# Key weights by rows, three centred tiles and other places for the bulk loads in a transformer block's forward and backward pass

## The chip, the cores and the metric

The kernel runs on one core of a Trainium2 chip. The metric is the device time of one execution in microseconds. The core has five engines that run their own instruction streams and meet at semaphores: PE (TensorE, matmuls; its weight loads are listed as PEld), DVE (VectorE), ACT (ScalarE), POOL (GpSimd) and SP (SyncE, which here only issues transfers). Transfers are issued from SP, ACT and POOL and are moved by 16 DMA engines. A "transposing load" is a transfer that turns a matrix on its way.

## The reference

The reference computes a block of linear attention followed by a gated MLP, and the gradients of all its inputs. With x of 2048 rows and 640 columns, 32 heads of 20 columns and F = 1728:

```python
ln = layernorm(x)                         # no weights
q, k, v = split(ln @ wqkv)                # 640 x 1920
phi(t) = where(t > 0, t + 1, exp(t)) + 1e-6
kv = sum_s phi(k)_s v_s ;  z = sum_s phi(k)_s          # per head
o = phi(q) kv / (phi(q) z + 1e-6)
h = x + o @ wo
out = h + (silu(layernorm(h) @ w1) * (layernorm(h) @ w3)) @ w2
return out, and the gradients of x, wqkv, wo, w1, w3, w2 for a given grad_out
```

All inputs and outputs are bfloat16.

## The kernel before

Rows are worked on in 16 tiles of 128 (S = 16 x 128), columns in 5 tiles of 128. There is no scheduler: the order of the instructions on each engine is the order in which the program calls them, and an engine that waits holds up all that stands behind it. SP's order of transfers is fixed in the same way.

*Loads at the start.* `load_x(a, b)` loads x tiles a to b - 1 into `x_sb`, `load_wq(a, b)` loads columns 320 a to 320 b of wqkv (2 to 4 are the key weights, 0 to 2 the query weights, 4 to 6 the value weights). SP issues x 0, x 1, the first half of the key weights, x 2, the second half, x 3, x 4-5 (L115, L189 to L195), then w2 and grad_out by transposing loads (`load_w2T`, `load_g2T`, L460 and L461), x 6-9 (L462) and more.

*Pass one* (the loop at L528) takes the 16 tiles in turn. The layer norm of a tile is two BN_STATS, an aggregate and an addition on DVE (`Stats.part`, `stat`), a power on POOL (the reciprocal deviation `ln_rs`) and then the normalisation in place: on DVE (`ln1.norm`, L161), or for tiles 10, 12 and 14 on ACT (`norm_act`, L166), which also needs a bias made on POOL (L170). Tile 0 is only centred (`center_first`); its reciprocal deviation is applied as a scale in the activations (`RAW = 1`) and, later, to `x_sb` itself by `p1_scale` (L264). The tile is turned by PE transposes with a copy by ACT (`p1_tr`, tiles 0 to 7) or by a transposing load (tiles 8 to 15, issued in `p1_norm`, L251). Then PE multiplies it with the key weights: two halves of 320 columns, 5 matmuls each (`p1_half`, L268), into an accumulator `big` of which there are two. ACT takes Exp and Relu of it (`phi`, L295 and L296) into `mq` and `rq`, of which there are three each; DVE makes the feature from them (L299, L300) and thus frees them. This last step (`rest`) is kept in a list and runs later, where `v_steps` has an `R`. After tiles 6, 7, 9 and 11 query tiles 0 to 3 are made in the same way (`q_tile`).

`v_steps` is the order of DVE's work by tile: `S` statistics, `N` normalisation, `C` scaling, `R` rest; they come ahead of the tile's `phi`. `A`, `B` and `L` are normalisations after it: `A` before the query tile, `B` and `L` behind it. `trickle` names the bulk loads (w1 and w3 in pieces, `w13`) that are issued at the end of a tile, `outs` the stores. `m_part` accumulates phi(k)^T times x in spare places (L430), `ghh_chunk` makes pieces of grad_out times w2^T (L395).

*After the loop* the rest of the query tiles, the denominators (`r_prod` on POOL; `r_head` = `r_row` on DVE and `r_T`, a transposing load) and kv alternate, with bulk loads between them (L592 to L624). The list of `run` (L948) then makes Wp (the folded kv times wo, five transposing loads, L709) and the attention output by tile (`f2_half`, L657). `r_store` (L735) stores scaled queries with transfers issued from POOL.

*The backward pass* ends the weight gradient of wo in `q_parts` (L1219 to L1226), whose last products `tri` are turned by transposing loads and used at L1388. Around it SP issues `load_xnT` (the normalised x, turned, 4 pieces), `load_wqT` (wqkv turned), and at L1402 to L1415 the loads of `mN` and `pkb`. The remaining stages up to 818 us are matmuls in which PE is not held up.

Of the kernel before, what the change touches and what calls it, by code (L numbers as in the profile page):

```python
# [55 lines left out]
def kernel(  # L56
# [126 lines left out]
    def load_wq(a, b):  # L183
        dma(out=wqkv[:, :, a * HD:b * HD], in_=wq_v[:, :, a * HD:b * HD])

    def load_x(a, b):
        dma(out=x_sb[:, a:b, :], in_=xS[:, a:b, :])

    load_x(1, 2)  # L189
    A.activation(sg[:], zero[:], AF.Exp)  # L190
    load_wq(2, 3)
    load_x(2, 3)
    load_wq(3, 4)
    load_x(3, 4)
    load_x(4, 6)  # L195

# [45 lines left out]
    RAW = 1  # L242
# [23 lines left out]
    def p1_half(acc, t, n0):  # L266
        for c in range(DT):
            T.matmul(acc, lhsT=pqT[:, c, t * P:(t + 1) * P], rhs=wqkv[:, c, n0:n0 + HD], start=(c == 0),  # L268
                     stop=(c == DT - 1))

    def p1_acc():
        return ps.tile([P, 2, 512], F32, name="big", bufs=2)

    def p1_mm(t, n0, between=None, halves=None):
        acc = p1_acc() if halves is None else None
        for j in range(2):
            p1_half(acc[:, j, 0:HD] if halves is None else halves[j][:, 0:HD], t, n0 + j * HD)
            if j == 0 and between is not None:
                between()
        return acc  # L280
# [6 lines left out]
    def phi_tiles():  # L287
        return [p1.tile([P, D], BF16, name=n, bufs=3) for n in ("mq", "rq")]

    def phi(acc, dst, t, parts=None):  # L290

        mq, rq = parts or phi_tiles()
        if parts is None:
            kw = dict(scale=ln1.rs[:, t:t + 1]) if t < RAW else {}
            A.activation(two(mq[:]), acc[:, :, 0:HD], AF.Exp, **kw)  # L295
            A.activation(two(rq[:]), acc[:, :, 0:HD], AF.Relu, **kw)  # L296

        def rest():
            V.tensor_scalar(out=mq[:], in0=mq[:], scalar1=1.0, scalar2=1e-6, op0=ALU.min, op1=ALU.add)  # L299
            V.tensor_tensor(out=dst, in0=mq[:], in1=rq[:], op=ALU.add)  # L300
        held.append(rest)
# [160 lines left out]
    load_x(6, 10)  # L462
# [26 lines left out]
    warm_up(8, p1_acc()[:, 0])  # L489
    stat(1)  # L490
    p1_norm(1)
    ln1.part(x_sb, 2, 0)
    ln1.part(x_sb, 2, 1)
    ln1.part(x_sb, 3, 0)
    p1_norm(2)
# [7 lines left out]
    def load_wo():  # L503
        dma(out=wo[:], in_=A_wo.rearrange("(c p) n -> p c n", p=P))

    trickle = {4: w13[0], 5: lambda: w13[1](0, 1), 6: lambda: w13[1](1, 2), 12: w13[2]}
# [3 lines left out]
               4: (("S", 7), R, ("N", 7), ("S", 8)), 5: (R, ("N", 8), ("S", 9)), 6: (R, ("N", 9), ("S", 10)),  # L510
               7: (("S", 11), R, R, ("A", 10), ("L", 11)), 8: (("S", 12), R, R, ("S", 13)),
               9: (("N", 13), R, ("S", 14), ("B", 12)), 10: (R, R, ("S", 15)), 11: (R, ("A", 14), ("L", 15))}
# [15 lines left out]
    for t in range(ST):  # L528
        first = None
        if t < RAW:  # L530
            first = phi_tiles()
            kh = [ps.tile([P, 512], F32, name="k0", tag="m", bufs=2) for _ in range(2)]

            def act(i, j):
                A.activation(first[i][:, j * HD:(j + 1) * HD], kh[j][:, 0:HD], (AF.Exp, AF.Relu)[i],
                             scale=ln1.rs[:, t:t + 1])

            def between():
                act(0, 0)
                p1_tr(t + 1)  # L540
                act(1, 0)
            k = p1_mm(t, D, between, kh)
            act(0, 1)
            act(1, 1)
        else:
            k = p1_mm(t, D, (lambda: p1_tr(t + 1)) if t + 1 < XT_DMA else None)
        steps = v_steps.get(t, (R,) * len(held))
        for step in steps:
            if step is R:
                held.pop(0)()  # L550
            elif step[0] in V_OPS:
                V_OPS[step[0]](step[1])
        phi(k, pk_all[:, t, :], t, first)
        for when in ("A", "B", "L"):
            for step in steps:
                if step is not R and step[0] == when:
                    p1_norm(step[1])
            if when == "A" and t in QT:
                q_tile(QT.index(t))
        if 3 <= t < 7:  # L560
            ghh_chunk(t - 3, lambda: ps.tile([P, 512], F32, name="gp", tag="m", bufs=2))
        m_part(0, M0.get(t, ()))
        if t >= 11:
            V.memset(bd[:, t - 11, :], 0.0)
            make_mask(t - 11)
        if t >= 9:
            m_part(1, [2 * (t - 9), 2 * (t - 9) + 1])
        for f, *n in outs.get(t, ()):
            f(*n)
        if t in trickle:  # L570
            trickle[t]()
# [10 lines left out]
    def r_head(t):  # L582
        r_row(t)
        r_T(t)
# [7 lines left out]
    load_wq(4, 6)  # L592
    group_out(SC - 1)
    w13[3]()
# [8 lines left out]
    load_wo()  # L603
    for go in w13[4:]:
        go()
# [6 lines left out]
    r_head(1)  # L612
# [9 lines left out]
    m_end(3)  # L622
    r_T(2)
    load_w2T(4 * P, 8 * P)  # L624
# [319 lines left out]
    def kv3():  # L944
# [6 lines left out]
        (q_out, 10, 14), (mlp_ghh, 4),  # L951
        (q_late, 15), (w2_room,), (sig_table,), (f2_half, 0, 0), (f2_half, 1, 0), (f2_half, 2, 0), (f2_half, 3, 0), (mlp_ghh, 5),
        (f2_half, 0, 1), (r_store, 4, 5), (f2_half, 1, 1), (f2_hn, 0), (r_store, 5, 6), (f2_half, 2, 1), (f2_hn, 1),
# [360 lines left out]
    part(4)  # L1314
    load_xnT(2)
    part(20)
# [64 lines left out]
    load_xnT(3)  # L1381
    load_wqT(0)
# [20 lines left out]
    dma(out=mN, in_=m_v)  # L1403
    dma(out=rows(dwoT_d), in_=dwoT[:])

# [8 lines left out]
    for n in range(4):  # L1414
        load_pk(n)  # L1415
# [189 lines left out]
```

## Time and profile before

| | |
|---|---|
| Median of 3 runs | 819.58 us (819.23 to 820.79) |
| The profiled execution | 820.36 us |
| Its span on the core | 818.6 us |
| PE busy | 811.6 us (99%) |
| DVE, ACT, POOL busy | 452.7, 324.8, 131.7 us |
| DMA moved | 162.46 MB, mean 198 GB/s |

By stretch, from the same execution (engine-busy time in us):

| Stretch | PE | DVE | ACT | GB/s |
|---|---|---|---|---|
| 5 to 16 us | 10.12 of 11 | 9.29 | 9.34 | 278 |
| 16 to 28 us | 11.95 of 12 | 11.21 | 10.56 | 279 |
| 28 to 46 us | 18.00 of 18 | 15.73 | 13.96 | 191 |
| 46 to 80 us | 34.00 of 34 | 24.79 | 20.47 | 267 |
| 80 to 100 us | 19.57 of 20 | 17.51 | 13.47 | 218 |
| 558 to 568 us | 9.53 of 10 | 1.90 | 1.90 | 165 |

A profile line of the timeline holds the start in us from the span's start, the duration in us, the engine, the line of the kernel, the operation, what it writes and reads, the size, the number of instructions taken together (xN), and in brackets the engine's idle time before it and what ended it. "SPq" is SP's sequencer issuing transfers. In the list of waits the numbers are the total in us, the number of times and the longest. Matmuls are pipelined, so a line's duration runs past the start of the next; the pace is read from starts: 0.135 us for a matmul 320 wide.

### The profile page before, as it was taken

How to read it: one execution, taken by the hardware profiler on the slowest of the kernel's cores; microseconds unless marked ns; L12 is line 12 of the kernel's file. 1: busy time of each engine (PE TensorE's matmuls, PEld its weight loads, DVE VectorE, ACT ScalarE, POOL GpSimd, SP SyncE). 2: the span in 40 equal slices, each digit the busy share in tenths (PEclk: the TensorE clock that was granted, in tenths of full speed). 3: DMA queues.
4: the chain of work that ended last, by engine and by line, in shares of the span. 5: the costliest groups of instructions: out<-in, count | busy, mean ns of one | idle time of the engine just before them, and what ended most of it. 6: DMA issues, size and time to landing. Idle time of an engine off the chain costs nothing.

```text
span 818.6 us, 13711 instructions
## 1 busy us (share of the span) xinstructions
PE 811.6 (99%) x5261; PEld 501.6 (61%) x5292; DVE 452.7 (55%) x973; ACT 324.8 (40%) x609; POOL 131.7 (16%) x198
## 2 busy tenths in 40 slices
PE   9999999999999999999999999999999999999998
PEld 6777544555555555754577777777777777544444
DVE  7859997998898566300057777772781544200000
ACT  7856688665565666011112212222212334211111
POOL 2243333323222212100001111110220000000000
PEclk9999999999999999999999999999999999999999
DMA  9899899696485556999877877269994888979991
GB/s 262 207 242 277 206 276 302 207 244 174 128 209 158 169 168 168 239 254 243 233 178 181 218 194 193 58 111 181 269 217 93 179 193 153 249 175 235 221 239 37
DMA packets 335889, 162.46 MB, mean 198 GB/s; under 512 B 252560, under 2 KB 329072, under 8 KB 335824
## 3 DMA queue, kind: packets, MB, share of 16 engines
q1 hardware_dynamic: 291920, 120.68, 63.8%
q0 software_dynamic: 7328, 24.48, 8.9%
q10 hardware_dynamic: 36576, 16.42, 8.2%
q8 instruction: 41, 0.67, 0.3%
q14 instruction: 24, 0.20, 0.1%
HBM read 47.09 MB, written 53.43 MB: 123 GB/s over the span
## 4 chain that ended last, share of the span: by engine, by line
PE 96%; DMA 1%; ACT 1%; DVE 1%; issue 0%; SPq 0%; POOL 0%; DVEq 0%
PE mm L395 20%; PE job L1335 19%; PE ghn L1131 14%; PE gxn L1504 8%; PE gw L1086 7%; PE big L268 4%; PE o L913 4%; PE o L859 3%; PE gwo L1219 3%; PE macc L430 3%; PE gr L1188 3%; PE dkv L1441 3%; PE at L657 2%; DMA wqkv<-in_A_wqkv_dram 1%; PE dkv L1369 1%; DMA tri<-tri 1%
## 5 line engine op out<-in xcount | busy, mean ns | idle before, releaser
L1335 PE MATMUL job<-gb,hnN 128*128 128x496 bf16 (+3 forms) x576 | 116.8, 366 | 0.0
L1131 PEld LDWEIGHTS <-ggb 128*128 128x128 bf16 x864 | 84.5, 98 | 33.0
L395 PE MATMUL mm<-pqT,w 128*128 128x512 bf16 x396 | 93.2, 379 | 0.5
L1335 PEld LDWEIGHTS <-hnN 128*128 128x128 bf16 x576 | 55.8, 98 | 61.0
L395 PEld LDWEIGHTS <-w 128*128 128x128 bf16 x540 | 52.6, 98 | 62.9 <-issue 0.6
L1339 ACT CAST obs<-job 128x496 bf16<-128x496 f32 (+4 forms) x56 | 28.5, 510 | 123.6 <-PE job L1335 123.6
L1131 PE MATMUL ghn<-w13a,ggb 128*128 128x320 bf16 x448 | 63.5, 299 | 0.0
L1146 DVE SCALAR_TENSOR_TENSOR wb<-gs,hnb 128x640 f32<-128x640 bf16 x16 | 13.2, 825 | 88.1 <-ACT gs L1143 88.1
L1131 PE MATMUL ghn<-w13b,ggb 128*128 128x320 bf16 x416 | 61.4, 299 | 0.0
L395 PE MATMUL mm<-g2T,w2T 128*128 128x512 bf16 x228 | 58.8, 379 | 0.6
L1086 PE MATMUL gw<-hb,g 128*128 128x512 bf16 (+2 forms) x316 | 58.4, 345 | 0.2
L1086 PEld LDWEIGHTS <-g 128*128 128x128 bf16 x320 | 31.3, 98 | 27.0
L420 ACT CAST ghh<-mm 128x512 bf16<-128x512 f32 x48 | 28.2, 588 | 48.2 <-PE mm L395 41.4
L1196 POOL TENSOR_TENSOR sz<-Zb,g_h 128x640 f32<-128x640 bf16 x16 | 20.2, 1262 | 163.7 <-DVE g_h L1197 163.7
L796 ACT ACTIVATE sig<-mm 128x512 bf16<-128x512 f32 x56 | 33.7, 602 | 25.0 <-PE mm L395 21.6
L1143 ACT ACTIVATE gs<-ghn 128x640 bf16<-128x640 f32 x16 | 11.3, 705 | 76.0 <-PE ghn L1131 76.0
L395 PEld LDWEIGHTS <-w2T 128*128 128x128 bf16 x260 | 25.4, 98 | 23.4
L268 PEld LDWEIGHTS <-pqT 128*128 128x128 bf16 x320 | 30.7, 98 | 13.5 <-ACT pqT L260 0.9
L268 PE MATMUL big<-wqkv,pqT 128*128 128x320 bf16 x250 | 38.4, 299 | 0.2
L1335 PEld LDWEIGHTS <-g 128*128 128x128 bf16 x320 | 31.0, 98 | 11.5
L832 DVE TENSOR_TENSOR gate<-gate,sig 128x1024 bf16<-128x1024 bf16 x28 | 19.3, 689 | 33.9 <-ACT gate L807 31.1
L1091 ACT CAST gw2o<-gw 128x512 bf16<-128x512 f32 (+2 forms) x20 | 10.4, 519 | 66.6 <-PE gw L1086 25.3
(217 smaller groups left out, 1391.2 us busy)
## 6 DMA issues: line engine op xcount, KB each, us to landing
hh_d<-hhT SPq DMA_DIRECT2D x24, 256.0 KB, 2.8
gg_d<-gate POOLq DMA_DIRECT2D x24, 256.0 KB, 4.4
gg_d<-ghh POOLq DMA_DIRECT2D x24, 256.0 KB, 4.1
ggb<-gg_d SPq DMA_DIRECT2D x6, 896.0 KB, 5.3
ggb<-gg_d ACTq DMA_DIRECT2D x6, 832.0 KB, 5.7
ggb<-gg_d SPq DMA_DIRECT2D x2, 1728.0 KB, 13.9
pk_d<-pk_all SPq DMA_DIRECT2D x4, 640.0 KB, 5.4
g<-in_grad_out_dram SPq DMA_DIRECT2D x4, 640.0 KB, 5.7
```

The source lines that it names most:

```text
L268: T.matmul(acc, lhsT=pqT[:, c, t * P:(t + 1) * P], rhs=wqkv[:, c, n0:n0 + HD], start=(c == 0), stop=(c == DT - 1))
L395: T.matmul(acc[:], lhsT=w[:, c, fc * P:(fc + 1) * P], rhs=rhs[:, c, :], start=(c == 0), stop=(c == DT - 1))
L420: A.copy(out=ghh[n // 2][:, n % 2, :], in_=acc[:])
L430: T.matmul(macc[m][j][:, 0:n], lhsT=pk_all[:, t, m * P:(m + 1) * P], rhs=x_ext[:, t, j * HD:j * HD + n], start=(t == 0), stop=(t == ST - 1))
L796: A.activation(sig[:, i, :], gp[:], AF.Sigmoid)
L859: T.matmul(accs[i, j][:, 0:HD], lhsT=hhT[c][:, fc, i * P:(i + 1) * P], rhs=w2[:, fc, j * HD:(j + 1) * HD], start=(first and fc == 0), stop ...
L913: T.matmul(o2["ps"][:, 0:HD], lhsT=hhT[c][:, fc, i * P:(i + 1) * P], rhs=w2[:, fc, j * HD:(j + 1) * HD], start=(fc == 0), stop=(fc == FT - 1))
L1086: T.matmul(acc[:, 0:fw], lhsT=g2[:, t, m * P:(m + 1) * P], rhs=hb[b][:, t, 0:fw], start=(t == 0), stop=(t == ST - 1))
L1131: T.matmul(acc[:, j, 0:HD], lhsT=ggb[t // 2][:, k, lo:lo + P], rhs=rhs[:, j * HD:(j + 1) * HD], start=(k == 0), stop=(k == NG - 1))
L1335: T.matmul(acc[:, 0:n], lhsT=lhs[:, t, m * P:(m + 1) * P], rhs=rhs(t), start=(t == 0), stop=(t == ST - 1))
L1339: A.copy(out=ob, in_=acc[:, 0:n])
L1504: T.matmul(acc[:, j, 0:HD], lhsT=g, rhs=wqT[:, k, j * HD:(j + 1) * HD], start=(k == 0), stop=(k == 14))
```

## The change

It has seven parts.

1. The key weights come in two pieces by rows (256 and 384 rows of 640 columns; `load_wk`), both ahead of x tile 2. Tile 0's product is made row piece by row piece (`first_mm`); four warm-up matmuls after tile 0's transposes instead of eight. Tile 0's activations are taken whole.
2. Tiles 1 and 2 too are only centred (`RAW = 3`), and scaled on DVE later (`("C", 1)` and `("C", 2)` at tiles 5 and 6). In tile 1 the transposes of the next tile come after both halves (`at`).
3. x tiles 6 to 9 are loaded ahead of the transposing loads of w2 and grad_out.
4. The normalisations of tiles 12 and 14 on ACT come ahead of the activations of tiles 9 and 11 (`F`).
5. Bulk loads move: w1's second piece from tile 12 to tile 7, the value weights to tile 9, w3's second piece to tile 13, wo and the rest of w1 and w3 to the end of the loop, the second piece of w2 to where those were.
6. Query tile 1's transposing load comes after those of m's last block; r's tiles 4 and 5 are stored earlier from POOL.
7. In the backward pass the third and fourth pieces of the turned x and the query part of the turned wqkv are loaded later: behind the transposing loads of `tri`, and behind `pkb`.

```diff
+    def load_wk(a, b):
+        dma(out=wqkv[:, a:b, D:2 * D], in_=wq_v[:, a:b, D:2 * D])
     load_x(1, 2)
     A.activation(sg[:], zero[:], AF.Exp)
-    load_wq(2, 3)
+    load_wk(0, 2)
+    load_wk(2, DT)
     load_x(2, 3)
-    load_wq(3, 4)
     load_x(3, 4)
     load_x(4, 6)
+    load_x(6, 10)
...
-    RAW = 1
+    RAW = 3
...
+    def p1_mm(t, n0, between=None, at=0):
+        acc = p1_acc()
         for j in range(2):
+            p1_half(acc[:, j, 0:HD], t, n0 + j * HD)
+            if j == at and between is not None:
                 between()
         return acc

+    def first_mm(between):
+        acc = p1_acc()
+        for c in range(DT):
+            for j in range(2):
+                T.matmul(acc[:, j, 0:HD], lhsT=pqT[:, c, 0:P], rhs=wqkv[:, c, D + j * HD:D + (j + 1) * HD],
+                         start=(c == 0), stop=(c == DT - 1))
+            if c == 1:
+                between()
+        return acc
...
     load_g2T(0)
-    load_x(6, 10)
     load_w2T(2 * P, 4 * P)
...
-    warm_up(8, p1_acc()[:, 0])
-    stat(1)
-    p1_norm(1)
+    warm_up(4, p1_acc()[:, 0])
+    ln1.part(x_sb, 1, 0)
+    ln1.part(x_sb, 1, 1, lambda: center(1))
     ln1.part(x_sb, 2, 0)
-    ln1.part(x_sb, 2, 1)
+    ln1.part(x_sb, 2, 1, lambda: center(2))
     ln1.part(x_sb, 3, 0)
-    p1_norm(2)
     ln1.part(x_sb, 3, 1)
...
-    trickle = {4: w13[0], 5: lambda: w13[1](0, 1), 6: lambda: w13[1](1, 2), 12: w13[2]}
+    trickle = {4: w13[0], 5: lambda: w13[1](0, 1), 6: lambda: w13[1](1, 2), 7: w13[2], 9: lambda: load_wq(4, 6), 13: w13[3]}
...
-               4: (("S", 7), R, ("N", 7), ("S", 8)), 5: (R, ("N", 8), ("S", 9)), 6: (R, ("N", 9), ("S", 10)),
+               4: (("S", 7), R, ("N", 7), ("S", 8)), 5: (R, ("N", 8), ("S", 9), ("C", 1)), 6: (R, ("N", 9), ("S", 10), ("C", 2)),
                7: (("S", 11), R, R, ("A", 10), ("L", 11)), 8: (("S", 12), R, R, ("S", 13)),
-               9: (("N", 13), R, ("S", 14), ("B", 12)), 10: (R, R, ("S", 15)), 11: (R, ("A", 14), ("L", 15))}
+               9: (("F", 12), ("N", 13), R, ("S", 14)), 10: (R, R, ("S", 15)), 11: (("F", 14), R, ("L", 15))}
...
+        turn = (lambda: p1_tr(t + 1)) if t + 1 < XT_DMA else None
+        k = p1_mm(t, D, turn, int(t == 1)) if t else first_mm(turn)
...
+            elif step[0] == "F":
+                p1_norm(step[1])
...
-    load_wq(4, 6)
     group_out(SC - 1)
-    w13[3]()
+    load_wo()
+    for go in w13[4:]:
+        go()
     z_late((2, 3, 4), big())
...
-    load_wo()
-    for go in w13[4:]:
-        go()
+    load_w2T(4 * P, 8 * P)
...
-    r_head(1)
+    r_row(1)
...
+    r_T(1)
     r_T(2)
-    load_w2T(4 * P, 8 * P)
...
-        (q_out, 10, 14), (mlp_ghh, 4),
+        (r_store, 4, 5), (q_out, 10, 14), (r_store, 5, 6), (mlp_ghh, 4),
...
-        (f2_half, 0, 1), (r_store, 4, 5), (f2_half, 1, 1), (f2_hn, 0), (r_store, 5, 6), (f2_half, 2, 1), (f2_hn, 1),
+        (f2_half, 0, 1), (f2_half, 1, 1), (f2_hn, 0), (f2_half, 2, 1), (f2_hn, 1),
...
     part(4)
+    part(20)
     load_xnT(2)
-    part(20)
...
-    load_xnT(3)
-    load_wqT(0)
     fill(4)
...
-    dma(out=mN, in_=m_v)
-    dma(out=rows(dwoT_d), in_=dwoT[:])
...
-    for n in range(4):
-        load_pk(n)
+    load_pk(0)
+    load_pk(1)
+    dma(out=mN, in_=m_v)
+    dma(out=rows(dwoT_d), in_=dwoT[:])
+    load_pk(2)
+    load_pk(3)
+    load_xnT(3)
+    load_wqT(0)
```

More of the change, by code (lines that the diff above doesn't have):

```diff
@@ L272, in p1_acc @@
         return ps.tile([P, 2, 512], F32, name="big", bufs=2)
-    def p1_mm(t, n0, between=None, halves=None):
-        acc = p1_acc() if halves is None else None
+    def p1_mm(t, n0, between=None, at=0):
+        acc = p1_acc()
         for j in range(2):
-            p1_half(acc[:, j, 0:HD] if halves is None else halves[j][:, 0:HD], t, n0 + j * HD)
-            if j == 0 and between is not None:
+            p1_half(acc[:, j, 0:HD], t, n0 + j * HD)
[9 more added lines that the diff above has]
+            if c == 1:
                 between()
@@ L288, in phi_tiles, with phi @@
         return [p1.tile([P, D], BF16, name=n, bufs=3) for n in ("mq", "rq")]
[L290 to L296, printed above, removed]
+    def phi(acc, dst, t):
+        mq, rq = phi_tiles()
+        kw = dict(scale=ln1.rs[:, t:t + 1]) if t < RAW else {}
+        A.activation(two(mq[:]), acc[:, :, 0:HD], AF.Exp, **kw)
+        A.activation(two(rq[:]), acc[:, :, 0:HD], AF.Relu, **kw)
         def rest():
@@ L528 @@
     for t in range(ST):
[L529 to L546, printed above, removed]
+        turn = (lambda: p1_tr(t + 1)) if t + 1 < XT_DMA else None
+        k = p1_mm(t, D, turn, int(t == 1)) if t else first_mm(turn)
         steps = v_steps.get(t, (R,) * len(held))
@@ L550 @@
                 held.pop(0)()
+            elif step[0] == "F":
+                p1_norm(step[1])
             elif step[0] in V_OPS:
                 V_OPS[step[0]](step[1])
-        phi(k, pk_all[:, t, :], t, first)
+        phi(k, pk_all[:, t, :], t)
         for when in ("A", "B", "L"):
```

## The prediction

> **What bounds the kernel now.** I read the busy shares and the chain first, then the waits of PE, then timelines of the stretches that the change touches.
>
> ```profile
> PE 811.6 (99%) x5261; PEld 501.6 (61%) x5292; DVE 452.7 (55%) x973; ACT 324.8 (40%) x609; POOL 131.7 (16%) x198
> PE 96%; DMA 1%; ACT 1%; DVE 1%; issue 0%; SPq 0%; POOL 0%; DVEq 0%
> ...
> PE k L268 <- DMA wqkv<-in_A_wqkv_dram: 0.6, 2, 0.4
> PE gkvT L1388 <- DMA tri<-tri: 0.5, 1, 0.5
> PE at L657 <- DVE rden L378: 0.2, 1, 0.2
> ```
>
> PE is the bound. The change neither adds nor removes a real matmul, so it can only win where PE waits, and every microsecond by which PE is pushed back is lost for good. Waits are few: about 1.5 us before 13.5 us (two for key weights, three for a transposed x tile), 0.40 at 85.57 us and 0.63 at 566.50 us (both taken between the starts of neighbouring matmuls, which is more than the idle time in the list). That is some 2.5 us to win in 819. L657 is put down to DVE, but PE's weight loader waited there until 85.52 for a Wp block that landed at 85.48.
>
> The start, from the timeline:
>
> ```profile
> 6.61 0.84 PE L268 MATMUL k<-wqkv,pqT 128*128 128x320 bf16 x5 [0.18 <-DMA wqkv<-in_A_wqkv_dram]
> 8.14 0.84 PE L268 MATMUL k<-wqkv,pqT 128*128 128x320 bf16 x5 [0.41 <-DMA wqkv<-in_A_wqkv_dram]
> ...
> 10.94 0.45 DVE L161 TENSOR_SCALAR x_sb<-x_sb,ln_mv,ln_rs 128x640 bf16<-128x640 bf16 x1 [0.26 <-POOL ln_rs L155]
> ```
>
> See that PE waits for both halves of the key weights, and that DVE normalises tile 3 only at 10.94: PE's tile 3 starts at 12.68, and from 10.94 on DVE has no gap over 0.11 us until 35.06.
>
> Tiles 8 to 12 of pass one, ACT, POOL, DVE and PE:
>
> ```profile
> 29.15 0.70 ACT L295 ACTIVATE mq<-big 128x640 bf16<-128x640 f32 x1 [0.20 <-DVE pk_all L300]
> ...
> 32.40 0.70 ACT L295 ACTIVATE mq<-big 128x640 bf16<-128x640 f32 x1 [0.76 <-DVE pk_all L300]
> ...
> 34.84 0.92 ACT L166 ACTIVATE x_sb<-x_sb,nb,ln_rs 128x640 bf16<-128x640 bf16 x1
> ...
> 32.21 0.41 POOL L170 TENSOR_SCALAR nb<-ln_mv,ln_rs 128x1 f32<-128x1 f32 x1
> ...
> 18.16 0.38 DVE L264 TENSOR_SCALAR x_sb<-x_sb,ln_rs 128x640 bf16<-128x640 bf16 x1
> 18.46 0.88 DVE L148 BATCH_NORM_STATS2 st<-x_sb 128x6 f32<-128x320 bf16 x2
> ...
> 30.74 2.88 PE L268 MATMUL big<-wqkv,pqT 128*128 128x320 bf16 x20
> 34.27 1.52 PE L268 MATMUL big<-wqkv,pqT 128*128 128x320 bf16 x10
> 39.98 1.25 PE L268 MATMUL big<-wqkv,pqT 128*128 128x320 bf16 x8
> ```
>
> PE has no wait here, but little room. ACT's Exp waits for DVE (a pair of feature buffers of the three must be free), and PE's next tile needs the accumulator of two tiles before, of which there are two. Tile 9's Exp and Relu end at 33.70, PE wants that buffer at 34.27; the pair before it ends at 30.45 against 30.74; tile 11's ends at 39.79 against 39.98.
>
> **The change part by part.**
>
> *Start.* The two 400 KB column halves become row pieces of 320 and 480 KB, both ahead of x tile 2. Before, landing times were: x1 3.60, first half 6.57, x2 7.00, second half 8.10, x3 8.53, x4-5 9.38. At the same place in bytes x2 now lands where the second half did, 8.10. The first half took 2.97 us after x1, the second only 1.10 after x2: 1.87 us are no data time. If that excess goes with the rows of the first weight transfer (256 for 640), x2 lands at 8.10 - 1.87 x 0.6 = 6.98. Nothing here says which; I take 7.4, a bit nearer the low end, since all later transfers are then in a backlog as the second half was. The Trainium skill ("DMA: Bandwidth & Descriptors", Specifications) puts full transfer rate at pieces of 512 B and up, so rows of 640 and 1280 B would differ in nothing. By that rule x2 lands at 8.10 and the sum below is 0.70 higher; the trace agrees on the steady rate (400 KB in 1.10, 320 KB in 0.85 us) and is silent on the excess.
>
> From x2 on the work is a chain: two statistics 0.92 with the gap, aggregate 0.24, centring 0.45 (the row of the 640-wide normalisation; its step is 0.36), two statistics of x3 0.92, aggregate and epsilon 0.4, POOL's power 0.65 with its gaps, which hides x4's first statistics, normalising x3 0.45, then to PE's transposes, ACT's copy (starts 0.49 later, 0.69) and tile 3: with overlaps 5.36 us. So tile 3 starts at 7.4 + 5.36 = 12.76 against 12.68: **+0.08**. Centring instead of normalising spares tile 2 the wait for POOL, but x2 is 0.4 later. Tile 0's product by rows, the half as many extra warm-up matmuls and tile 1's transposes after both halves lie inside this chain (PE would be ready for tile 3's transposes about 0.4 earlier). ACT's four half activations of tile 0 become two whole ones; hidden.
>
> *x 6 to 9 ahead of the transposing loads.* SP issues it at about 4.3 instead of 10.81 and everything behind moves. The first transposed gradient landed at 12.78, wanted at 14.44. 640 KB more ahead of it cost 1.7 us at the steady rate, so 14.0 to 14.5 against 14.5: nothing, or up to 0.3. What is late next would be the DVE chain, so I take 0.
>
> *Two more scalings on DVE* (tiles 1 and 2, at steps 5 and 6): 0.30 each, from 18.16 to 18.46. DVE has no gap there, so all behind shifts by 0.60. The pair ending 30.45 (query tile 1) also gets a scale operand (the Exp with ln_rs took 0.79, without 0.70): 0.60 + 0.18 gives 31.23, PE wanted 30.74: **+0.53** with 0.04 of signal.
>
> *Normalisation of tiles 12 and 14 first on ACT.* It now stands ahead of tile 9's Exp and waits for POOL's bias, 32.62 + 0.60 = 33.22. It takes 0.92, so the Exp that started at 32.40 starts at 34.06 and its Relu ends at 35.36; PE wants 34.27 + 0.53 = 34.80: **+0.60**. Tile 14 likewise: bias 38.76 + 0.60, normalised by 40.31, tile 11's pair ends at 41.50, PE wants 39.98 + 1.13 = 41.11: **+0.43**. What the earlier normalisations buy is two earlier transposing loads, and no matmul waited for those.
>
> *Bulk loads.* Moved on SP: w1 rows 256 to 511 to step 7, the value weights to step 9, w3's to step 13, wo and the rest to the end of the pass, w2's 512 to 1023 to about 60 us; tile 1's transposing load goes past them. They pass the transposing loads of tiles 12 to 15. In 28 to 46 us the queue moves 191 GB/s of the 370 it reached, so cover is there: tile 12's landing rises to about 38.9, wanted at 41.5. If the cover is gone, see the rivals. In return, the stretch from 72 us is free of w2's load (SP busy with it 72.77 to 75.96), x 0 to 5 start about 0.8 sooner, and the third Wp block, which landed at 85.48, needs only the 2.6 us of an unhindered transposing load after its issue at 82.39. That is 85.0; PE is there at 85.17: **-0.40**. The two stores of r go earlier on POOL (0.59 each), behind products, into idle time: 0.
>
> *Around 562 us.*
>
> ```profile
> 558.77 3.34 SPq L1242 DMA_TRANSPOSE xnT<-xn_d  x1
> 560.76 0.69 ACT L1222 CAST tri<-gwo 128x640 bf16<-128x640 f32 x1 [3.73 <-PE gwo L1219]
> 562.21 1.22 SPq L1226 DMA_TRANSPOSE tri<-tri  x1
> 566.50 0.72 PE L1388 MATMUL gkvT<-tri,woT 128*128 128x140 bf16 x9 [0.47 <-DMA tri<-tri]
> ```
>
> The last tri block is ready at 561.47, waits behind xnT's 3.34 us issue and then lands 4.2 us after its own. Issued first it lands in 2.6, at 564.2; PE wants it at 565.87: **-0.63**. The loads put behind (two of xnT, wqT) are wanted about 600 us or later. wqT's five blocks now queue behind them, some 2 to 5 us later, and PE wants them at 625; SP idles from 608 to 615, which covers it.
>
> **Sum.** +0.08 + 0.53 + 0.60 + 0.43 - 0.40 - 0.63 = +0.61. The profiled execution took 820.36 us (span 818.6, 1.76 around), 0.78 above the median of the three runs, so 820.97 for it and **820.2** for the median of 819.58.
>
> **The rivals.** 0.2%, 1.64 us, is about what a measurement of this kernel can tell from no change.
>
> - *Room in tiles 8 to 12 (faster).* If DVE's lag is not what holds ACT, the 1.56 us there are nothing: 818.6; with x2 landing at 6.2 (all 1.87 of excess gone), 817.5. For it: DVE waits 0.67 at 35.06, so something else paces it there. Against it: four Exps in a row are released by DVE, and that wait is for POOL, which is late itself when DVE is. Chance 0.25, of which 0.17 is past 1.64.
> - *The bulk loads hold up the x transposes (slower).* Place: tiles 12 and 14. w1's load took 9.43 us to land in its old place; issued at 33.2 it would land at 42.6, tile 12's block 0.7 later, 1.8 after PE wants it. It decides from a landing of 41.5 on. With half of that again at tile 14, where the value weights took 6.3 us, 822 to 823. Against it: the old place was behind two stores of 640 KB, the new one behind one. Chance 0.15.
> - *PE's clock comes late (slower).* The first matmuls (128 wide) start 0.106 apart, from about 6.2 us 0.055. The granted-clock column says 1.00 throughout and doesn't show it. With four warm-ups fewer and idle time before the second weight piece, it may come only after tile 1: 20 matmuls of 0.135 at 1.93 times that lose 2.5, less 0.4 of room: 822.3. It decides if full pace comes after 8 us. The Trainium skill ("TensorE: Matmul & The Clock Gate", Part 1) has the clock granted after a busy window of about 3.4 us that runs freely, and taken after an idle one. No gap here is that long, so by that rule it holds. Chance 0.05.
> - *The waits at 85 and 566 stay.* Then 821.2. The two depend on transfers that are plainly in front. Chance 0.05.
>
> **How the numbers follow.** Forecast 0.50, within 819.4 (x2 early) to 821.0 (x2 at 8.10). Faster by over 0.2%: 0.17. Slower: 0.12 of the bulk loads, 0.05 of the clock, 0.03 of the last rival: 0.20. Within: 0.63. The range, 817.4 to 821.9, takes in the first rival and leaves out most of the slower ones.
>
> **What would show it.** x2's first statistics at 7.4 and tile 3's matmuls near 12.8; ACT idle about 1 us ahead of tile 12's L166, which now precedes an Exp; PE's list of waits with new entries for L268 released by ACT between 30 and 42 us, 1.5 in all; no wait at L657 and none for tri. I am wrong if L268 has no such waits, if x2 lands before 7, or if PE waits for a pqT transposing load.

## The result, and the profile after

| | before | changed |
|---|---|---|
| Median of 9 executions | 819.58 us | 823.07 us |
| Lowest and highest | 819.22, 821.41 us | 822.03, 830.45 us |
| Profiled execution (span) | 820.36 us (818.6) | 822.03 us (820.3) |

The change costs time: the ratio is 1.0055 (95% interval 1.0034 to 1.0076), 3.5 us by the medians. Forecast were 820.2 us and a range of 817.4 to 821.9. The changed kernel's times also spread more than those of before. In the table of experiments two stray executions, of 3686 us (e7) and 1744 us (e8), are left out of the ranges and the ratios; the medians count them.

Busy shares and chain of the changed kernel:

```profile
PE 812.8 (99%) x5288; PEld 501.0 (61%) x5288; DVE 452.9 (55%) x975; ACT 325.6 (40%) x607; POOL 131.7 (16%) x198
...
PE 94%; DVE 3%; DMA 1%; ACT 1%; issue 0%; SPq 0%; POOL 0%; DVEq 0%; ACTq 0%
```

PE is the bound as before. Its waits (total, times, longest, us):

```profile
...
PE at L653 <- DMA pqT<-pql: 0.9, 1, 0.9
PE big L272 <- ACT pqT L264: 0.8, 1, 0.8
PE big L272 <- ACT rq L309: 0.7, 2, 0.5
PE big L290 <- DMA wqkv<-in_A_wqkv_dram: 0.6, 2, 0.4
PE gp L408 <- DMA g2T<-in_grad_out_dram: 0.4, 1, 0.4
...
```

Line numbers have moved (L268 is L272, L657 is L653, L395 is L408, L385 is L398). The two waits for `rq` are two of the three forecast ones. The wait for `pqT` from ACT stands at 10.70 us, ahead of tile 2, inside the chain from x tile 2 to tile 3 that the prediction adds up. Those for `g2T` (the transposed gradient) and for `pqT<-pql` (r's tile 4, transposed) were costed at nothing. The same places in the timeline, tile 12 first:

```profile
33.56 0.92 ACT L166 ACTIVATE x_sb<-x_sb,nb,ln_rs 128x640 bf16<-128x640 bf16 x1 [0.89 <-POOL nb L170]
34.39 0.68 ACT L308 ACTIVATE mq<-big 128x640 bf16<-128x640 f32 x1
34.97 0.69 ACT L309 ACTIVATE rq<-big 128x640 bf16<-128x640 f32 x1
...
35.71 1.52 PE L272 MATMUL big<-wqkv,pqT 128*128 128x320 bf16 x10 [0.48 <-ACT rq L309]
...
8.07 4.03 SPq L230 DMA_TRANSPOSE g2T<-in_grad_out_dram  x1
...
15.24 1.02 PE L408 MATMUL gp<-g2T,w2T 128*128 128x512 bf16 x4 [0.39 <-DMA g2T<-in_grad_out_dram]
```

ACT idles 0.89 us for POOL's bias, normalises tile 12, and only then takes tile 9's Exp; PE stands until its Relu is done. The gradient's transposing load lands at 15.20 (12.78 before). Between 86 and 96 us:

```profile
87.41 0.60 POOL L731 DMA_DIRECT2D r_d<-pql  x1
88.01 0.76 POOL L724 DMA_DIRECT2D pq_d<-pkx  x1
88.38 4.47 SPq L398 DMA_TRANSPOSE pqT<-pql  x2
88.76 0.55 POOL L731 DMA_DIRECT2D r_d<-pql  x1
...
95.04 0.85 PE L653 MATMUL at<-Wp,pqT 128*128 128x320 bf16 x5 [0.86 <-DMA pqT<-pql]
```

Three stores from POOL stand around the issue of r's tile 4, which lands at 95.00, 6.62 us after its issue (4.32 before). And at the tri products, which no longer wait:

```profile
557.49 7.52 SPq L1222 DMA_TRANSPOSE tri<-tri  x3
565.05 3.12 SPq L1238 DMA_TRANSPOSE xnT<-xn_d  x1
...
567.23 1.73 PE L1382 MATMUL gkvT<-tri,woT 128*128 128x140 bf16 x25
```

Below, PE's loss at a place is taken between the starts of neighbouring matmuls, less the usual pace, as in the prediction.

### The profile page after: what moved, and what is told of

Read it like the earlier page. It is cut to its first block, busy times and chain, and to the rows that moved or that the text cites. A ratio compares the mean times of both kernels' runs of the same rounds, so it can differ in the third digit from the quotient of the medians.

```text
span 820.3 us, 13738 instructions
## 1 busy us (share of the span) xinstructions
PE 812.8 (99%) x5288; PEld 501.0 (61%) x5288; DVE 452.9 (55%) x975; ACT 325.6 (40%) x607; POOL 131.7 (16%) x198
## 4 chain that ended last, share of the span: by engine, by line
PE 94%; DVE 3%; DMA 1%; ACT 1%; issue 0%; SPq 0%; POOL 0%; DVEq 0%; ACTq 0%
PE mm L408 20%; PE job L1331 20%; PE ghn L1127 14%; PE gxn L1501 8%; PE gw L1082 7%; PE o L909 4%; PE o L855 3%; PE gwo L1215 3%; PE gr L1184 3%; PE dkv L1438 3%; PE macc L443 2%; PE at L653 2%; PE big L272 2%; DVE st L148 1%; PE mm L272 1%; DMA pqT<-pql 1%
## 5 line engine op out<-in xcount | busy, mean ns | idle before, releaser
L408 PE MATMUL mm<-pqT,w 128*128 128x512 bf16 x405 | 93.6, 379 | 0.0
L408 PEld LDWEIGHTS <-w 128*128 128x128 bf16 x540 | 52.6, 98 | 63.1 <-issue 0.9
L408 PE MATMUL mm<-g2T,w2T 128*128 128x512 bf16 x240 | 59.6, 379 | 0.0
L408 PEld LDWEIGHTS <-w2T 128*128 128x128 bf16 x260 | 25.4, 98 | 24.0 <-issue 0.6
L272 PE MATMUL big<-wqkv,pqT 128*128 128x320 bf16 x250 | 38.2, 299 | 1.6 <-ACT pqT L264 0.8
L272 PEld LDWEIGHTS <-pqT 128*128 128x128 bf16 x310 | 29.7, 98 | 14.1 <-ACT pqT L264 1.4
```

What stands on the lines that cost most here:

```text
L408: T.matmul(acc[:], lhsT=w[:, c, fc * P:(fc + 1) * P], rhs=rhs[:, c, :], start=(c == 0), stop=(c == DT - 1))
```

## The experiments

All medians with what ran beside them on the same chip (us; ratio with its 95% interval):

| | kernel | median (range) | before beside it | ratio |
|---|---|---|---|---|
| e1 | changed, r's stores back | 822.83 (821.43 to 827.78) | 820.27 | 1.0035 (1.0020 to 1.0051) |
| e2 | changed, part 4 undone | 824.02 (822.92 to 825.81) | 820.27 | 1.0047 (1.0031 to 1.0062) |
| e3 | changed, x 6-9 back | 822.36 (822.07 to 832.10) | 819.86 | 1.0034 (1.0005 to 1.0063) |
| e4 | changed, part 7 undone | 822.73 (822.25 to 823.50) | 819.86 | 1.0031 (1.0021 to 1.0042) |
| e5 | before + part 7 | 820.75 (819.75 to 823.68) | 819.86 | 1.0001 (0.9984 to 1.0018) |
| e6 | before + w2 early | 823.91 (821.15 to 826.70) | 819.86 | 1.0041 (1.0019 to 1.0063) |
| e7 | before + part 4 | 820.66 (820.26 to 822.93) | 819.80 | 1.0015 (1.0005 to 1.0025) |
| e8 | before + parts 1, 2 | 821.31 (819.68 to 825.30) | 819.80 | 1.0018 (1.0004 to 1.0031) |
| e9 | before + bulk loads, tri first | 822.73 (821.94 to 826.47) | 819.80 | 1.0039 (1.0026 to 1.0053) |
| e10 | before + tri first | 822.11 (821.08 to 823.35) | 819.80 | 1.0028 (1.0016 to 1.0039) |
| e11 | changed, three things undone | 821.99 (820.81 to 829.89) | 819.99 | 1.0034 (1.0012 to 1.0057) |
| e12 | before + part 7, q_out from SP | 820.35 (819.84 to 823.36) | 819.99 | 1.0008 (0.9996 to 1.0020) |
| e13 | changed, again | 823.39 (822.11 to 830.33) | 819.99 | 1.0051 (1.0032 to 1.0071) |
| e14 | changed, wqT's second part later | 823.35 (822.30 to 825.45) | 819.61 | 1.0044 (1.0031 to 1.0056) |
| e15 | e12 + wqT's second part later | 820.09 (819.88 to 822.17) | 819.61 | 1.0007 (0.9998 to 1.0015) |
| e16, e17 | before, one profile each | 819.40, 819.33 | 820.73 | - |
| e18 | before + part 7, wqT's second part later | 821.07 (819.37 to 822.22) | 820.73 | 1.0002 (0.9993 to 1.0012) |

The theory I began with: the forecast steps hold, and two transfers that I had costed at nothing (g2T, r's tile 4) make the rest. Rivals: the key weights by rows, or the backward part.

### e1: r's stores at their old place

```diff
-        (r_store, 4, 5), (q_out, 10, 14), (r_store, 5, 6), (mlp_ghh, 4),
+        (q_out, 10, 14), (mlp_ghh, 4),
...
-        (f2_half, 0, 1), (f2_half, 1, 1), (f2_hn, 0), (f2_half, 2, 1), (f2_hn, 1),
+        (f2_half, 0, 1), (r_store, 4, 5), (f2_half, 1, 1), (f2_hn, 0), (r_store, 5, 6), (f2_half, 2, 1), (f2_hn, 1),
```

> The changed kernel with one thing undone: r's tiles 4 and 5 are stored from POOL at their old place, behind the first halves of the attention output. Theory: the changed kernel's longest new wait, 1.0 us at L653 at 95 us, is r's transposing load of tile 4 (issued 88.38, landed 95.00) sharing the DMA engines with these two stores and the scaled queries; then it lands within 4.5 us of its issue as before, the wait goes, and the median falls by about 1.0 us to 822.0. Rival: the transposing loads of Wp and the scaled queries alone make it late; then the wait stays and the time is 823. The scatter of the changed kernel's times (822 to 830) stays by both.

The wait at 95 us is gone; r's tile 4 lands 4.53 us after its issue. The median is 2.6 us above before beside it, where the changed kernel stands 3.5 above (3.4 in e13): 0.9 us less, as expected, though the intervals overlap. The profiled execution (826.22) shows where longer ones lose: 1.51 us for a late key weight piece at 7.97, three waits for rq (1.50 in all), and 3.08 us at 613.6, where DVE waits for `pkb`.

### e2: part 4 undone

The run's label speaks of the start; what it undoes is part 4:

```diff
-               9: (("F", 12), ("N", 13), R, ("S", 14)), 10: (R, R, ("S", 15)), 11: (("F", 14), R, ("L", 15))}
+               9: (("N", 13), R, ("S", 14), ("B", 12)), 10: (R, R, ("S", 15)), 11: (R, ("A", 14), ("L", 15))}
```

> The changed kernel with the normalisations of tiles 12 and 14 put back behind the activations of tiles 9 and 11. Theory: PE's two waits for rq (0.65 us at 35.7, 0.36 at 41.8) come from ACT doing tile 12's and 14's normalisation ahead of the Exp; without it at least 0.6 us of them goes and the median is 822.3. Rival: the two scalings on DVE hold ACT's Exp anyway; then PE waits for rq in another tile, 823.

Both missed: no wait for rq anywhere, and no gain (824.02, of 6 executions). In the profiled one g2T landed at 16.69, PE lost 2.44 us there, then ran at half pace from 17.5 to 20.9 us, and at 44.9 waited 0.97 us for tile 14's transposing load, which this edit makes later. Whether the waits for rq are gone by the edit or because PE came 2.4 us late, this profile doesn't show: with part 4 in place, e4 and e13 have none either behind waits of 2.10 and 1.87 us for g2T, but e14 has 1.37 us behind one of 2.06.

### e3: x 6 to 9 back behind the transposing load

```diff
-    load_x(6, 10)
...
     load_g2T(0)
+    load_x(6, 10)
```

> The changed kernel with x tiles 6 to 9 loaded behind the transposing load of grad_out again, as before. Theory: with them ahead, that load lands at 15.20 instead of 12.78 and in some executions later (16.69 in the profile of the last experiment, where PE stood for 2.4 us and its matmuls from 18.1 to 21 us then took twice the time): this is 0.55 us of the changed kernel's profiled execution and most of what its slower executions lose. Then the load lands by 14.0, PE doesn't wait for it, the median falls by 1 to 2 us to 821.0 to 822.0 and the highest times come down by 2.5 or more. Rival: the key weights by rows or the backward part make the spread; then the median is 822.5 and the highest times stay over 825.

g2T lands at 12.30 without a wait. Over all profiles here it landed at 15.20 to 17.09 in the six with x 6 to 9 ahead, and at 12.30 to 13.04 in the fourteen others. The median is 2.5 us above before beside it, 1 us less than the changed kernel's, but 0.4 above the theory's range, and 828.87 and 832.10 stayed. More is not won because ACT's waits are then all there, and two waits for Wp with them, in the timeline of e3:

```profile
30.98 2.88 PE L271 MATMUL big<-wqkv,pqT 128*128 128x320 bf16 x20 [0.38 <-ACT rq L308]
...
35.11 1.52 PE L271 MATMUL big<-wqkv,pqT 128*128 128x320 bf16 x10 [0.43 <-ACT rq L308]
...
41.25 0.97 PE L271 MATMUL big<-wqkv,pqT 128*128 128x320 bf16 x6 [0.27 <-ACT rq L308]
...
86.95 2.89 PE L653 MATMUL at<-Wp,pqT 128*128 128x320 bf16 x20 [0.35 <-DMA Wp<-pkx]
...
91.92 0.85 PE L653 MATMUL at<-Wp,pqT 128*128 128x320 bf16 x5 [0.87 <-DMA Wp<-pkx]
```

From start to start the waits for rq cost 0.54, 0.60 and 0.44: 1.57, where the prediction's steps gave 0.53, 0.60 and 0.43. Those for Wp cost 0.51 and 1.03. At the second of them the fifth Wp block took 4.94 us from its issue at 86.93, with POOL's three stores issued at 86.89 to 88.24: here this block comes late, and r's tile 4 isn't waited for. Together with the earlier tile 3 (-0.27) the waits come to 2.8 us; this execution (822.11) is 2.7 above those of e16 and e17.

### e4: part 7 undone

The diff of part 7 backwards.

> The changed kernel without part 7 (the loads around the tri products in their old order). Theory: part 7 brings the 0.63 us at the tri products, but puts the loads of the turned wqkv and of pkb together later, and in some executions PE stands for up to 3 us at 613 us because pkb is late (one such in the first experiment). Then the wait of 0.6 us for tri is back, no wait stands between 600 and 640 us, and the median is within 0.5 of 823, with a smaller spread at the top. Rival: part 7 is a plain gain; the median rises by 0.6 to 823.7 and the spread stays.

The spread at the top went (822.25 to 823.50, 10 executions) and nothing waits between 600 and 640 us, as expected. But the wait for tri did not come back: the first sign that it isn't usual. g2T cost 2.10 us, r's tile 4 1.13.

### e5 to e9: parts alone

e5 is before with part 7, e7 with part 4 (the v_steps line above, the other way, with `N` for `F`), e8 with parts 1 and 2, each as in the diff of the change.

> The kernel before with part 7 alone. By the step of the prediction: 0.63 us less, 818.95. Rival, the late pkb: the wait for tri is gone, but some executions are 1 to 4 us longer than the kernel before, and the median is not below 819.6.

No gain (0.9984 to 1.0018). The profiled execution lost 1.43 and 0.78 us to Wp blocks that land late.

> The kernel before with part 4 alone: the normalisations of tiles 12 and 14 ahead of the activations of tiles 9 and 11. By the steps of the prediction, without the 0.60 us of scalings: the pair of tile 9 ends at 34.84 where PE wants it at 34.27 (0.57), that of tile 11 at 40.90 for 40.58 (0.32): two waits for rq, 0.9 us in all, and the time 0.9 us above the runs of before beside it. Rival: ACT has the room, since its idle time ahead of the Exp is as long as the normalisation: no wait, same time.

The theory held: 0.60 us at 34.94 and 0.30 at 40.95, 0.9 us as worked out (0.57 + 0.32), and a median 0.86 us up. Both waits are for `rq` (at 40.95 the Relu ends at 40.90).

> The kernel before with parts 1 and 2 alone (key weights by rows, three centred tiles). Theory: tile 3 starts about 0.3 us earlier, as in the third experiment, and the two scalings cost one wait for rq at 31 us of 0.53; without part 4 nothing else: 0.2 us above the runs of before beside it. Rival: the 0.60 us of DVE lag go on and PE waits again at 35 and 41 us, 1.5 in all, so 1.2 us above.

The wait at 32 us was 0.55 and there was none at 35 and 41, as expected. But the median rose by 1.5 us, lowest to lowest by 0.4: in the profiled execution (822.53) the second weight piece landed at 7.83, tile 3 began at 13.52, and PE lost 1.10 and 0.41 us to Wp blocks, which this edit doesn't touch. Over the nine profiles with weights by rows, tile 3 began at 12.38 to 13.61 (mean 12.92); before, at 12.62 and 12.67 in e16 and e17.

e6 moves only w2's second piece and query tile 1's transposing load:

```diff
+    load_w2T(4 * P, 8 * P)
     dmaG(out=m_v[:, 0, :], in_=mbs[:, 0, :])
...
-    r_head(1)
+    r_row(1)
...
+    r_T(1)
     r_T(2)
-    load_w2T(4 * P, 8 * P)
```

> The kernel before with the second piece of w2 loaded at about 60 us instead of 72, and query tile 1's transposing load behind those of m's last block; nothing else. By the step of the prediction: the wait of 0.40 us for a Wp block at 85.57 goes, 819.2. Rival: the gain is taken back at 95 us by a transposed r tile that lands late; then the same time as before, with a wait at L657 there.

Neither: the median is 4 us up (6 executions). The profiled execution, the shortest of them (821.15), has no wait for Wp, but one in another place. SP and PE in the timeline of e6:

```profile
63.51 7.82 SPq L457 DMA_TRANSPOSE w2T<-in_B_w_dram  x1
...
72.75 1.22 SPq L442 DMA_TRANSPOSE mT<-hx  x1
...
76.63 1.11 PE L449 MATMUL kv<-mT,wqkv 128*128 128x160 bf16 x15 [1.17 <-DMA mT<-hx]
```

The issue of w2's load holds SP for 7.82 us, m's transposing load behind it goes out at 72.75 instead of 69.91 (e16), and PE loses 1.33 us; a wait for tri costs 0.56 more. What the longer executions lose isn't seen. In the changed kernel, where the other bulk loads have left this place, that wait doesn't exist.

e9 takes all bulk loads and the tri products' new place, without part 4 (two of its hunks):

```diff
-    trickle = {4: w13[0], 5: lambda: w13[1](0, 1), 6: lambda: w13[1](1, 2), 12: w13[2]}
+    trickle = {4: w13[0], 5: lambda: w13[1](0, 1), 6: lambda: w13[1](1, 2), 7: w13[2], 9: lambda: load_wq(4, 6), 13: w13[3]}
...
-    load_xnT(2)
     part(20)
+    load_xnT(2)
```

> The kernel before with part 5 (bulk loads), query tile 1's transposing load behind those of m, and of part 7 only that the tri products stand ahead of the third piece of the turned x; nothing of the start, of part 4 and of r's stores. By the steps of the prediction 0.40 + 0.63 less: 1.0 us below the runs of before beside it. Rival: the transposing loads of tiles 12 to 15 or of Wp come late among the moved loads: no gain or a loss of 1 to 3 us, with a wait for pqT between 40 and 47 us or for Wp between 85 and 92.

The rival, in full (tiles 12 and 14, timeline of e9):

```profile
40.99 1.53 PE L268 MATMUL big<-wqkv,pqT 128*128 128x320 bf16 x10 [0.85 <-DMA pqT<-x_sb]
...
46.36 1.53 PE L268 MATMUL big<-wqkv,pqT 128*128 128x320 bf16 x10 [0.84 <-DMA pqT<-x_sb]
```

1.01 and 1.00 us, and 1.09 more at 587.7. So part 4 is the price of part 5: with the loads moved, tiles 12 and 14 must be normalised early, for 0.9 us, or be late, for 2.0.

### e10: the tri products first, alone

The last hunk of e9.

> The kernel before with only one thing of part 7: the tri products and their transposing loads ahead of the third piece of the turned x. Theory: the wait of 0.63 us at 566 goes and nothing is moved towards 590 to 615 us, so 0.6 us below the runs of before beside it, without a longer tail. Rival: the third piece, which is now some 5 us later, makes its users wait: same time.

Worse by 2.3 us by the medians (7 executions); the profiled execution (821.08) is the shortest. The third piece of the turned x and all behind it go later on SP; pkb, wanted by DVE, lands at 584.44, against 578.89 and 580.57 in e16 and e17 (timeline of e10):

```profile
584.53 0.83 DVE L1445 SCALAR_TENSOR_TENSOR g_k<-pkb,gp 128x640 bf16<-128x640 bf16 x1 [2.86 <-DMA pkb<-pk_d]
...
586.34 1.52 PE L1441 MATMUL dkv<-small,xnT 128*128 128x320 bf16 x10 [1.47 <-DVE gp L1444]
```

PE loses 1.63 us. That is why part 7 puts pkb ahead as well, and its price in turn is a late wqT (e13).

### e11, e12: the collisions out of the way

e11 is the changed kernel with the edits of e1 and e3 and, as e12 (before with part 7), with

```diff
     def q_out(a, b):
-        dmaG(out=pq_v[:, a:b, :], in_=pkx[0][:, DT + a - 10:DT + b - 10, :])
+        dma(out=pq_v[:, a:b, :], in_=pkx[0][:, DT + a - 10:DT + b - 10, :])
```

> The changed kernel with x 6 to 9 back behind grad_out's load, r's two stores at their old place, and the scaled queries (q_out) stored from SP, behind r's transposing loads, where POOL issued them among the last Wp block and those loads. Theory: the sum of the prediction holds for the rest, and the excess is the two collisions. From the profiles: tile 3 0.3 us earlier (third experiment), three waits for rq 1.57, no wait at Wp (-0.40), none at tri (-0.63), none over 0.3 us between 85 and 96 us: 0.24 us above the runs of before beside it, and below the changed kernel by 2 us. Rival: the lateness of loads is spread over the whole change; then it stays 2 us or more above before, with a wait for Wp, pqT or pkb.

> The kernel before with part 7, and the scaled queries stored from SP behind r's transposing loads instead of from POOL. Theory: in the fifth experiment (part 7 alone) the 0.63 us at tri were gained and hidden by two waits for Wp, the second (0.78) by a fifth block that took 5.5 us with q_out issued just ahead of it, against 2.6. Without that collision the fifth block takes 2.6 to 2.7 us, r's tile 4 under 4, and the time is 0.6 us below the runs of before beside it. Rival: it is the first Wp blocks, late behind w2's load, that spread the times; then no gain over the fifth experiment, 0.2 to 0.9 us above before.

The collisions went as foreseen: r's tile 4 took 3.03 and 2.57 us, Wp's fifth block 2.58 and 2.69. The times didn't follow: 2.0 and 0.36 us above before. e11's profiled execution has the three waits for rq (1.58) and one of 2.44 us for pkb at 612; e12's waits 0.86 us at Wp and 0.51 for m's transposing load. In e11's profile the waits for rq, the later tile 3 (0.31) and 0.43 us more at the end of the program (last section) come to 2.3 us without pkb, and by this estimate a median 2.0 above before leaves about 0.3 of the 1.03 us of gains. So I doubted the starting point.

### e13, e14: the changed kernel again, and wqT's second part later

> The changed kernel itself beside the two, for a second profile of it and times of the same chip. Theory: 3 to 3.5 us above the runs of before beside it, with g2T landing after 15 us and r's tile 4 taking over 6 us from issue to landing. Rival: the excess belongs to one chip; then under 2 us.

3.4 us above before: it is no matter of one chip. The profiled execution took 829.59. Its waits:

```profile
PE dkv L1438 <- DVE gp L1441: 4.2, 1, 4.2
PE gp L408 <- DMA g2T<-in_grad_out_dram: 1.7, 1, 1.7
...
PE at L653 <- DMA pqT<-pql: 0.9, 1, 0.9
...
PE big L272 <- DMA pqT<-x_sb: 0.5, 1, 0.5
```

and the stretches around the first of them (us, PE, PEld, DVE, ACT and POOL busy with counts, granted clock, DMA share, GB/s):

```profile
600.00:615.30 15.30, 11.18 (x92) 8.16 (x90) 9.55 (x13) 1.76 (x4) 2.36 (x4) 0.95 1.24 152
615.30:620.60 5.30, 5.25 (x20) 2.99 (x20) 4.39 (x6) 0.00 (x0) 0.54 (x1) 0.50 1.19 190
620.60:630.00 9.40, 9.40 (x71) 6.75 (x70) 0.00 (x0) 1.71 (x4) 0.54 (x1) 1.00 1.05 239
```

pkb's piece 6 landed at 613.45 (598.16 and 599.68 in e16 and e17). PE stood 4.3 us, and then the granted clock was 0.50 for 5.3 us: 20 matmuls at 0.267 us instead of 0.135, 2.6 us more. Part 7 had put wqT's second part, a transposing load under way from 596 to 615.5, on top of pkb's last pieces. From issue to landing piece 6 took 5.7 to 16.8 us in the eight profiles with this order, and 4.8 to 9.1 us in the twelve others.

```diff
-        if t == 2:
+        if t == 12:
             load_wqT(1)
```

This goes behind the transposing loads of pk at that place in the loop (e14 on the changed kernel).

> The changed kernel with the key part of the turned wqkv (load_wqT(1)) issued behind the turned pk pieces, at tile 12 of that loop instead of tile 2, so that it is not under way when pkb's last pieces are loaded from POOL. Theory: with part 7 this load starts at 595 instead of 587 and makes pkb's piece 6 land at 604 to 613; a landing after some 608 holds DVE and PE, 2.4 us in one execution and 4.3 in another, where PE then ran at half pace for 5 us more. Then pkb's piece 6 lands by 605, no wait stands at L1438, the times over 825 are gone and the median falls a little, to 2.5 us above the runs of before beside it. Rival: the longest times come from grad_out's load at 15 us; then times of 826 to 830 stay.

pkb's piece 6 landed at 606.41 and nothing waited there, but six executions and a median no lower (3.7 us above before, where 2.5 was expected) don't show that the long times are gone for good. One profile doesn't show either that wqT's second part made the piece late: at the old place it landed within 8.0 us of its issue in three of the eight, where here it took 8.13. In this profile g2T landed at 17.09 and cost 2.06 us, with 1.37 for rq.

### e15 to e18: is there a gain at all?

e15 is e12 with e14's edit, e18 the same with `q_out` from POOL.

> The kernel before with part 7, the scaled queries stored from SP and load_wqT(1) at tile 12. Theory: 0.63 us less at tri, no wait for pkb, fewer at Wp: 0.5 us below the runs of before beside it. Rival: Wp's first blocks behind w2's load decide the times, or the turned wqkv is late at 627 us (a wait at L1501): no less than before.

0.5 us above before, though its profile has no wait at tri, none for pkb and one of 0.38 at Wp. Three executions of the old order (e4, e7, e8) had shown no wait at 566 either (e6 had one of 0.56), so before itself was profiled twice more.

> The kernel before itself, for a second profile. Theory: its profiled execution shown above, 820.36 us, is not the usual one: the waits of 0.40 us at 85.57 and 0.63 at 566.50, which the prediction books as gains, are not there in the usual execution of 819.3 (820.36 - 1.03 = 819.33). So this profile has neither wait, or lacks them by as much as it is shorter. Rival: both waits are there in an execution of 819.3 to 819.6, and the missing gain went elsewhere.

> The kernel before itself once more, a third profile, with the same expectations.

819.40 and 819.33 us. The waits of PE in e16, whole list, and SP around tri:

```profile
PE warm L468 <- DVE zero L125: 1.1, 1, 1.1
PE k L268 <- DMA wqkv<-in_A_wqkv_dram: 0.6, 2, 0.4
```

```profile
557.98 2.88 SPq L1242 DMA_TRANSPOSE xnT<-xn_d  x1
...
561.16 1.20 SPq L1226 DMA_TRANSPOSE tri<-tri  x1
...
564.59 1.73 PE L1388 MATMUL gkvT<-tri,woT 128*128 128x140 bf16 x25
```

Here xnT's issue takes 2.88 us instead of 3.34 and is over when the last tri block is ready at 561.13; the block lands in 2.61 us at 563.77, and PE doesn't wait. Nor does it at Wp (third block issued 82.21, landed in 2.66). In e17 both waits are absent too. The execution the prediction was read from had both, 1.03 us: 820.36 - 1.03 = 819.33. But e16 and e17 are short executions: on their chip the median of before was 820.73, the shortest 819.37; over all measurements here, 142 executions of before took 819.14 to 825.40, 819.99 in the middle. So the two profiles show what an execution of 819.4 lacks, and not what every other one lacks. The other profiles tell more. In the old order of part 7 the wait at 566 stood in two of seven (before and e6; not in e4, e7, e8, e16, e17). With w2's second piece at its old place, a wait of 0.38 to 1.43 us for the third Wp block stood in five of ten (before, e5, e8, e12, e15; not in e7, e10, e16, e17, e18).

> The kernel before with part 7 and load_wqT(1) at tile 12, the scaled queries stored from POOL as before. Theory: if the wait at 566 us is not in the usual execution of before, part 7 can't gain there, and repaired it costs nothing: within 0.3 us of the runs of before beside it (the 0.5 us of the last experiment were the six more semaphore waits of SP at the end of the program, 0.06 us each, and what stands around them). Rival: a gain of 0.6 us, with which this would beat both kernels.

The theory held: 0.34 us above before, ratio 0.9993 to 1.0012, with the rival's 0.6 us at the edge of the interval. Part 7, repaired, shows no gain. No version here beats before.

## Why the prediction was wrong

- **Tri (-0.63) and Wp (-0.40): the step that failed first.** Both waits were in the one profiled execution, 0.78 us above the median, and in neither of e16 and e17. The step "820.97 for it and 820.2 for the median" took them off the median too, as if every execution had them. An execution of 819.4 hasn't, and from there the prediction's own losses give 819.4 + 0.08 + 1.56 = 821.0. The mechanism of both steps was right: with w2 early and with tri first neither wait stands in the changed kernel's two profiles. What was wrong is how often they stand in before: tri in two of seven profiles, the third Wp block in five of ten.
- **r's stores on POOL ("into idle time: 0").** POOL was idle, the transfers it starts were not alone. From issue to landing, r's tile 4 took 2.6 to 3.0 us with no store from POOL near (e11, e12, e15), 4.2 to 4.6 with one (before and most others), 6.6 to 6.7 with three (changed, e2, e4, e13, e14; 5.4 in e3, where the first store was out earlier). Cost: 1.02 to 1.20 us at L653 in the five. e1, with two of the three stores gone from there, shows it: no wait. Its median is 0.9 us nearer to before, though the intervals overlap. In e3, where the stores were earlier, PE lost 1.03 us to Wp's fifth block instead.
- **x 6 to 9 ahead ("nothing, or up to 0.3").** I forecast 14.0 to 14.5; it was 15.20 to 17.09, and the waits were 0.55, 0, 2.44, 2.10, 1.87 and 2.06 (changed, e1, e2, e4, e13, e14). The 640 KB ahead were costed at the steady rate, 1.7 us; the landing came 2.4 to 4.3 us later than 12.78. The mean rate nearly held (250 to 271 GB/s from 3 to 16 us in these six, 267 in before), the order of landing did not: in e2 seven of the 16 engines were done with the load by 14.34 and the other nine at 16.57 to 16.69. Why isn't shown.
- **C scalings and F12, F14 (+0.53, +0.60, +0.43): right in mechanism and size.** 1.57 in e3, 0.90 in e7 against 0.89. Behind a wait for g2T they can be smaller: in the changed kernel's own profile 0.55 + 0.65 + 0.36 = 1.56, in e4 and e13 none is left behind 2.10 and 1.87; but e14 has 1.37 behind 2.06.
- **Start (+0.08).** x2 landed at 7.12 to 8.35, 7.57 in the mean, for 7.4; tile 3 at 12.92 in the mean, for 12.76. The chain between them held: 5.26 or 5.27 us in eight of nine profiles, for 5.36 (6.00 in e14, where x3 came late). What I missed is the spread of 1.2 us. By the Trainium skill's rule for full-rate pieces ("DMA: Bandwidth & Descriptors", Specifications), weighed in the prediction, x2 would land at 8.10: the spread holds both, so it isn't settled here.
- **The rivals.** "The bulk loads hold up the x transposes" is true without part 4 (e9). With it, tile 14 still waited 0.58 and 0.65 us in e4 and e13. The clock was not late at the start, as the rival had it, but lost behind waits (e2, e13). "The waits at 85 and 566 stay" missed the point: in a short execution they aren't there.

The profiled changed execution against the 819.37 of e16 and e17: tile 3 +0.28, g2T 0.55, rq 1.01, r's tile 4 1.02, and 0.18 in place of 0.25 at 96 to 100 us, 2.79 in all; measured 2.66. Longer executions add g2T's larger waits and pkb's (3.08, 2.44 and 4.34 us in three of eight profiles with part 7 and wqT's second part at tile 2). How often each occurs in executions without a profile, and why e5 has no gain at all where its profile lost the rest to Wp, stays open beyond that.

## What to carry to other kernels

A wait in one profiled execution is a gain only as far as the other executions have it too: when the profiled time stands above the median by about the sum of the waits you mean to remove, take more profiles first. A transfer moved into an idle stretch of the engine that issues it has to be costed for every transposing load that is under way with it (here 6.6 us to landing instead of 4.3). In this kernel, with PE at 99%, such moves came in chains (bulk loads need early normalisations, tri first needs pkb first, which makes wqT late), and each link cost at least as much as the first one was to win.

## What the runs showed of the hardware

- The granted clock was one half for 5.3 us behind a wait of 4.3 us (e13), and for 3.4 us behind one of 2.44 us (e2: 0.50 from 17.46 to 20.87), but stayed at 1.00 behind waits of 3.08 (e1) and 2.44 us (e11). So the length of a wait alone doesn't decide. The Trainium skill ("TensorE: Matmul & The Clock Gate", Part 1) has a window of about 3.4 us that runs freely, which fits that. It has the clock fall back after at least one idle window of that length; the 2.44 us of e2 would not have been enough, and there the measurement decides.
- With one store moved from POOL's queue to SP's, the time from the start of PE's last matmul to the end of the span was 3.34 to 3.36 us (e11, e12, e15) instead of 2.91 to 2.94: SP runs six more semaphore instructions of 0.06 us each after the last store has landed.
